# A gated linear-attention layer and its channel mixer on one core: cumulative decays move from PSUM to SBUF buffers, and the loads of later units' decays wait for a chunk's keys

## The chip, the core and the metric

The kernel runs on one core of a Trainium2 chip. The core has five engines that run side by side, each through its own list of instructions in order: TensorE (PE, matmuls; PEld is its weight load), VectorE (DVE), ScalarE (ACT), GpSimd (POOL) and SyncE (SP), which here issues all DMAs. They share SBUF; PE writes to PSUM, which DVE and ACT can read and write. The metric is the device time of one launch in microseconds (us). Before the change it was 357.06 us in the median of 3 runs (356.91 to 357.37).

## The reference

Batch 4, 8 heads, 768 steps, head width 48, so model width 384; the mixer's inner width is 1024. All in float32.

```python
f = 1.0 / (1.0 + np.exp(-f_logit))
for t in range(S):
    state = f[:, :, t, :, None] * state + np.einsum('bhd,bhe->bhde', k[:, :, t], v[:, :, t])
    y[:, :, t] = np.einsum('bhd,bhde->bhe', q[:, :, t], state)
...
x = y with the heads side by side
x_prev = x one step earlier (zero at the first)
xk = mu_k * x + (1.0 - mu_k) * x_prev
xr = mu_r * x + (1.0 - mu_r) * x_prev
k = np.maximum(xk @ w_k, 0.0)
v = k * k @ w_v
r = 1.0 / (1.0 + np.exp(-(xr @ w_r)))
return r * v
```

## The kernel before

**Chunks and units.** The 4 x 768 steps are cut into 24 chunks of 128 steps (index i) and 8 units of three chunks, 384 steps (index u). Attention goes chunk by chunk, the mixer unit by unit.

**Attention of chunk i** (`add_attention`). The steps have short names, which the text uses with the chunk's number behind them:

- `qk`, `v`: loads of queries with keys, and of values. `f{u}` loads the logits of a unit's decays (768 KB), `sf{u}` takes their sigmoid on ACT.
- `b`: a scan on DVE gives the running product of the decays within the chunk, 128 x 512 (L240). `bl` copies its last column. `ln`, `rb`: ACT takes its logarithm and the exponential of the negative, that is its reciprocal (L246, L248).
- `q`: q times b (L250). `kr`: k times the reciprocal, in two halves (L258, L259). `n`: reciprocal times b, which corrects the rounding of the reciprocal (L270). `k`: the corrected key, in three pieces (L262, L266).
- `TR`: PE transposes the keys into PSUM (L310); `kt` copies them to SBUF, on ACT (L314) or DVE (L315).
- `SP`: PE forms the scores and the chunk's sum of key times value (L325, L345). `m` copies the scores with the causal mask, on DVE (L337); for the first `AWAY` chunks ACT copies (L332) and `mg` on GpSimd masks (L334).
- `g`, `za`, `zb`, `T`: the state carried from chunk to chunk (L287 to L302). `YA`, `YB`: PE forms the output from the state and from the chunk (L362); `w` reads a marker between the two (L381, L382). `y` copies the output to SBUF (L394 on ACT, L396 on DVE), and `sp` spreads two heads' rows with small DMAs.

**Mixer of unit u** (`add_mix`). `d` is the difference of x and its predecessor (L464; for unit 0 two scaled copies on ACT, L474), `xm` the mix (L482; L477 for unit 0). Since PE multiplies with shortened numbers, every operand is split: `xh` is the rounded mix (L490 on ACT, L491 on DVE), `xl` the rest (L497, GpSimd). `F{u}.{f}`: eight groups of nine matmuls with W_k; `R{u}.{t}`: three with W_r; `W{u}.{t}{h}`: six of twelve matmuls with W_v (all L505). Between them `r` (relu, L528 or L529), `h` and `kk` (the square, rounded and exact), `l` (their difference, L543), `lg` and `sg` (the gate; `sg{u}` also takes the sigmoid of `f{u+3}` into the same buffer on ACT, between two table loads), `o` (the product) and `out`.

**Weights** (`add_words`). W_k, W_r and W_v come as 64-bit words in 8, 4 and 6 pieces. A piece is loaded, put together on DVE in three steps (`S` L623, `T` L632, `X` L635), rounded on ACT (`H` L638), and the rest taken on GpSimd (`L` L642). The W_v pieces pass through two buffers in turn, so piece 2 is loaded when piece 0 is done. `S` and `T` need a PSUM buffer in between.

**What sets the order.** All these steps are tasks with a place, one or several ways (an engine, an estimated duration) and the tasks they come after. `Plan.schedule` plays the program through with these estimates, picks at each turn the task that can start first (the smaller place on a tie) and the way that would end first, with a penalty for some engines (`DEAR`); it also puts in filler matmuls on PE (L700) where it expects PE to wait. What it yields is pinned: each engine's instructions stand in just this order. So a changed constant can move instructions on every engine. `BUFS` gives the number of buffers by tag. The tag `pm` has four PSUM buffers of 2 KB a partition; they serve `b`, `TR`, `d`, `F`, `R`, `W` and the weights' `S` and `T`. `NFB` = 3 buffers hold the decays `f`, `NQ` = 4 the queries and keys. `general` is a slow path for extreme data; it is not run here.

Of the kernel before, what the change touches and what calls it, by code (L numbers as in the profile page):

```python
# [52 lines left out]
SPLIT = True
HALVED = 1
PLACE = {"f1": -0.627, "f2": 0.21, "sf2": -1.016, "qk0": 0.854, "qk1": -0.278, "qk2": 0.127, "qk3": 0.31, "v0": -0.151, "v1": -0.224, "cst": 0.482, "mu": 0.138, "f3": -1.807}
CHECK = (2.0, 0.2)
DEAR = {"V": 2.498, "A": 2.512}


class Plan:  # L60
# [23 lines left out]
    def schedule(self, trace=None):  # L84
        free = {"P": 0.0, "V": 2.2, "A": 0.0, "G": 1.0, "Q": 0.7}
# [106 lines left out]
class Rwkv:  # L192


    wk = wr = wv = None
# [19 lines left out]
    def add_attention(self, pl, i):  # L215
        nc = self.nc
        u, c = divmod(i, UC)
        cs = i % NCH
# [5 lines left out]
        I = lambda name, j=i: [f"{name}{j}"] if j >= 0 and j % NCH in have.get(name, range(NCH)) else []  # L224
# [15 lines left out]
        pl.add(f"b{i}", ga, ("V", 1.25, 1, lambda: nc.vector.tensor_tensor_scan(  # L240
            b().rearrange(FL), f().rearrange(FL), self.low.rearrange(FL), 1.0, op0=ALU.mult, op1=ALU.max)),
            after=[f"sf{u}.{c}" if u == 0 else f"sf{u}"], takes=[("pm", ("b", i))])
        pl.add(f"bl{i}", ga, ("A", 0.2, 0, lambda: nc.scalar.copy(self.bl[:, i], b()[:, :, C - 1])),
               ("V", 0.15, 0, lambda: nc.vector.tensor_copy(self.bl[:, i], b()[:, :, C - 1])),
               uses=[("pm", ("b", i))])
        pl.add(f"ln{i}", ga, ("A", 0.63, 0, lambda: nc.scalar.activation(rb(), b(), AF.Ln)),  # L246
               after=["ex"], takes=[("rb", i)], uses=[("pm", ("b", i))])
        pl.add(f"rb{i}", ga, ("A", 0.63, 0, lambda: nc.scalar.activation(rb(), rb(), AF.Exp, scale=-1.0)),  # L248
               after=I("ln"), uses=[("rb", i)])
        pl.add(f"q{i}", ga, ("V", 0.69, 0, lambda: nc.vector.tensor_tensor(q(), q(), b(), op=ALU.mult)),  # L250
               after=I("qk"), uses=[("pm", ("b", i))])
# [18 lines left out]
        pl.add(f"n{i}", ga, ("V", 0.69, 0, lambda: nc.vector.tensor_tensor(b(), rb(), b(), op=ALU.mult)),  # L270
               after=I("rb") + I("q") + I("bl"), uses=[("pm", ("b", i)), ("rb", i)])
# [13 lines left out]
        if cs > 0:  # L285
# [3 lines left out]
            def state(e):  # L289
# [655 lines left out]
```

## Time and profile before

| | |
|---|---|
| median of 3 runs | 357.06 us (356.91 to 357.37) |
| the profiled execution | 357.22 us, of it 355.1 us the span of the instructions |
| instructions | 10862, of them 4482 matmuls |
| moved by DMA | 45.32 MB, mean 128 GB/s |
| granted PE clock over the span | 0.99 |

How to read it: the page gives each engine's busy time over the span, and the span in 40 slices of 8.9 us, where a digit is the busy share in tenths. A row of a timeline is: start, duration, engine, line, operation, output<-input, count, and in brackets how long the engine had been idle before and who ended that. A row of the groups is: line, engine, operation, tiles, count | busy us, mean ns of one | idle us just before them, and whom they waited for. In the chain that ended last a row is: start, duration, engine, tile, line; "issue" is time in which the engine waited for nothing that the profile shows. Line numbers are those of the kernel before; in the changed kernel the same statements stand one or two lines further down.

### The profile page before, as it was taken

How to read it: one execution, taken by the hardware profiler on the slowest of the kernel's cores; microseconds unless marked ns; L12 is line 12 of the kernel's file. 1: busy time of each engine (PE TensorE's matmuls, PEld its weight loads, DVE VectorE, ACT ScalarE, POOL GpSimd, SP SyncE). 2: the span in 40 equal slices, each digit the busy share in tenths (PEclk: the TensorE clock that was granted, in tenths of full speed). 3: DMA queues.
4: the chain of work that ended last, by engine and by line, in shares of the span. 5: the costliest groups of instructions: out<-in, count | busy, mean ns of one | idle time of the engine just before them, and what ended most of it. 6: DMA issues, size and time to landing. Idle time of an engine off the chain costs nothing.

```text
span 355.1 us, 10862 instructions
## 1 busy us (share of the span) xinstructions
PE 320.0 (90%) x4482; PEld 304.0 (86%) x4482; DVE 260.3 (73%) x526; ACT 201.5 (57%) x400; POOL 196.5 (55%) x235
## 2 busy tenths in 40 slices
PE   0294678999999999999999999999999999999993
PEld 0283567888989999999999999999999999999992
DVE  7887699989998798877999788848973943723110
ACT  3786358758367827844467537772676156605520
POOL 2555459985779357733677267725790634634400
PEclk9999899999999999999999999999999999999998
DMA  7999462336451363366323632131401100010001
GB/s 260 398 378 372 162 223 65 106 105 209 118 185 59 127 226 129 123 236 221 117 81 116 212 128 89 46 121 52 160 1 38 50 27 11 9 46 22 3 24 52
DMA packets 20650, 45.32 MB, mean 128 GB/s; under 512 B 2928, under 2 KB 13040, under 8 KB 20592
## 3 DMA queue, kind: packets, MB, share of 16 engines
q1 hardware_dynamic: 20592, 44.55, 37.0%
q8 instruction: 37, 0.61, 0.7%
q14 instruction: 21, 0.17, 0.1%
HBM read 38.64 MB, written 4.72 MB: 122 GB/s over the span
## 4 chain that ended last, share of the span: by engine, by line
PE 68%; DVE 13%; ACT 5%; issue 4%; DMA 3%; POOL 3%; SPq 1%; DVEq 0%; POOLq 0%; ACTq 0%
PE pm L505 55%; PE py L362 6%; PE pm L310 3%; PE pss L325 2%; DMA f<-in_zt 2%; DVE pm L632 2%; PE pss L345 2%; DVE pm L623 2%; POOL k2l L543 1%; DVE xm L482 1%; DVE ss L337 1%; DMA words<-in_wv 1%; DVE xm L477 1%; DVE words L635 1%; DVE xh L491 1%
## 5 line engine op out<-in xcount | busy, mean ns | idle before, releaser
L505 PE MATMUL pm<-xh,wk 128*128 128x384 f32 x384 | 105.3, 344 | 1.5 <-POOL wk L642 1.1
L505 PE MATMUL pm<-wv,k2h 128*128 128x384 f32 x384 | 98.6, 338 | 0.0
L543 POOL TENSOR_TENSOR k2l<-kk,k2h 128x384 fp32r<-128x384 f32 x64 | 68.5, 1075 | 32.2 <-DVE kk L535 16.3
L497 POOL TENSOR_TENSOR xl<-xm,xh 128x384 fp32r<-128x384 f32 x48 | 52.5, 1095 | 60.4 <-DVE xh L491 54.6
L505 PEld LDWEIGHTS pm<-xh,wk 128*128 128x128 f32 x384 | 69.8, 188 | 4.4 <-POOL wk L642 2.0
L505 PEld LDWEIGHTS pm<-wv,k2h 128*128 128x128 f32 x384 | 68.7, 188 | 0.3
L505 PE MATMUL pm<-xl,wk 128*128 128x384 f32 x192 | 64.6, 337 | 0.0
L505 PE MATMUL pm<-wv,k2l 128*128 128x384 f32 x192 | 64.5, 336 | 0.0
L528 ACT ACTIVATE r<-pm 128x384 f32<-128x384 f32 x54 | 26.5, 490 | 34.0 <-PE pm L505 33.3
L505 PE MATMUL pm<-wr,xh 128*128 128x384 f32 x144 | 38.0, 345 | 1.0 <-DVE words L635 0.9
L505 PEld LDWEIGHTS pm<-wv,k2l 128*128 128x128 f32 x192 | 36.1, 188 | 0.0
L595 DVE TENSOR_TENSOR o<-pm,lg 128x384 f32<-128x384 f32 x24 | 13.3, 553 | 31.1 <-PE pm L505 30.9
L505 PEld LDWEIGHTS pm<-xl,wk 128*128 128x128 f32 x192 | 36.1, 188 | 0.0
L535 DVE SCALAR_TENSOR_TENSOR kk<-pm,r 128x384 f32<-128x384 f32 x38 | 21.1, 554 | 20.0 <-ACT r L528 18.8
L533 ACT ACTIVATE k2h<-r 128x384 fp32r<-128x384 f32 x64 | 33.6, 524 | 3.5 <-DVE r L529 1.2
L240 DVE TENSOR_TENSOR_SCAN pm<-f,low 128x512 f32<-128x512 f32 x24 | 32.7, 1363 | 0.1
L362 PE MATMUL py<-qk,z 64*64 64x64 f32 x704 | 22.9, 230 | 10.0 <-issue 3.3
L362 PEld LDWEIGHTS py<-qk,z 64*64 64x64 f32 x704 | 16.4, 135 | 18.0 <-issue 8.8
L505 PEld LDWEIGHTS pm<-wr,xh 128*128 128x128 f32 x144 | 25.2, 188 | 1.9 <-DVE words L635 1.0
L482 DVE SCALAR_TENSOR_TENSOR xm<-pm,mu_sb,x 128x384 f32<-128x384 f32 x42 | 25.7, 612 | 0.7
L700 PE MATMUL py<-ident 128*128 128x64 f32 x72 | 10.8, 310 | 15.4 <-DMA ident<-in_cst 15.4
L505 PE MATMUL pm<-wr,xl 128*128 128x384 f32 x72 | 24.2, 336 | 0.0
(101 smaller groups left out, 559.2 us busy)
## 6 DMA issues: line engine op xcount, KB each, us to landing
qk<-in_qkt SPq DMA_DIRECT2D x24, 512.0 KB, 4.3
words<-in_wv SPq DMA_DIRECT2D x12, 512.0 KB, 3.9
f<-in_zt SPq DMA_DIRECT2D x7, 768.0 KB, 5.2
v<-in_vt SPq DMA_DIRECT2D x24, 192.0 KB, 3.1
out<-o SPq DMA_DIRECT2D x24, 192.0 KB, 2.6
words<-in_wk SPq DMA_DIRECT2D x6, 512.0 KB, 5.4
words_k2h<-in_wk SPq DMA_DIRECT2D x4, 384.0 KB, 8.6
words_k2l<-in_wk SPq DMA_DIRECT2D x4, 384.0 KB, 9.4
```

What stands on the lines that cost most here:

```text
L240: pl.add(f"b{i}", ga, ("V", 1.25, 1, lambda: nc.vector.tensor_tensor_scan(b().rearrange(FL), f().rearrange(FL), self.low.rearrange(FL), 1. ...
L310: nc.tensor.transpose(pk()[:, j], k()[:, j], self.ident)
L362: first[c, h] = nc.tensor.matmul(to, lhs, rhs, start=(c, h) not in first, stop=stop, skip_group_check=True)
L482: pl.add(f"xm{u}.{n}{j}", pr, ("V", 0.62, 0, lambda xm=xm, n=n, j=j: nc.vector.scalar_tensor_tensor(xm(), pm("d", u, j)[:, :UT], self.mu_s ...
L497: e.tensor_tensor(lo(), xm(), hi().bitcast(F32), op=ALU.subtract)
L505: nc.tensor.matmul(ps, lhs(a, j), rhs(bb, j), start=ends[0] and i == 0, stop=ends[1] and i == len(pr) - 1)
L528: pl.add(f"r{u}.{f}", kf, ("A", 0.5, 0, lambda r=r, ps=ps: nc.scalar.activation(r(), ps(), AF.Relu)), ("V", 0.56, 0, lambda r=r, ps=ps: nc ...
L533: pl.add(f"h{u}.{f}", kf, ("A", 0.53, 0, lambda r=r, hi=hi: nc.scalar.activation(hi(), r(), AF.Square)), after=[f"r{u}.{f}"], **kw)
L535: pl.add(f"kk{u}.{f}", kf, ("V", 0.56, 0, lambda r=r, ps=ps, kk=kk: nc.vector.scalar_tensor_tensor(kk(), ps(), 0.0, r(), op0=ALU.max, op1= ...
L543: e.tensor_tensor(lo(), kk(), hi().bitcast(F32), op=ALU.subtract)
L595: pl.add(f"o{u}.{t}", kv, ("V", 0.56, 0, lambda t=t, ps=ps, o=o: nc.vector.tensor_tensor(o(), ps(), lg()[:, t], op=ALU.mult)), after=[f"W{ ...
L700: self.nc.tensor.matmul(self.py[:, 0, 256:320], self.ident, self.ident[:, :64], start=False, stop=True, skip_group_check=True)
```

## The change

It does five things.

1. `b` leaves the PSUM buffers `pm` and gets three SBUF buffers of its own, tag `b`. Every step that reads or writes it follows: `bl`, `ln`, `q`, `n`, `k`.
2. The load `f{u}` for u >= 3 (whose buffer held the decays of unit u - 3) now also comes after `kt` of chunk 3(u - 3) + 4, that is after the keys of a chunk of the unit in between have been transposed and copied.
3. `q` and `n` may also be done by GpSimd. The planner counts `q`, `n` and `k` on DVE as steps that get in the way of GpSimd.
4. The planner's penalties: DVE 2.709 and ACT 2.426 (2.498 and 2.512 before), and 3.606 and 7.281 more for `q` and `n` on GpSimd. The score copies of the first four chunks instead of one go by ACT and GpSimd (`AWAY`).
5. Other constants of the planner: the distance at which attention leads the mixer, places of loads and of weight pieces, the chunk from which YA, SP and YB are tied together (`TIED` 7 instead of 8), and assumed delays.

```diff
 BUFS = {
-    "pm": (4, [512]), "rb": (2, [NP, C]),
+    "pm": (4, [512]), "b": (3, [512]), "rb": (2, [NP, C]),
...
-LEAD, GATE, PREP = 1.669, 0.274, 0.51
-WORDS = {"wk": (-0.282, 0.023), "wr": (-4.892, 0.005), "wv": (-0.241, 0.052)}
-HAND, DRAIN = 0.136, 0.465
+LEAD, GATE, PREP = 1.617, 0.274, 1.949
+WORDS = {"wk": (-0.422, 0.041), "wr": (-5.439, 0.054), "wv": (-0.301, 0.066)}
+HAND, DRAIN = 0.132, 0.301
...
-TIED = 8
+TIED = 7
...
-AWAY = 1
+AWAY = 4
...
-DEAR = {"V": 2.498, "A": 2.512}
+DEAR = {"V": 2.709, "A": 2.426, "qG": 3.606, "nG": 7.281}
...
-                pick = min(((max(at[w[0]], free[w[0]]) + w[1] + DEAR.get(w[0], 0.0), w) for w in ways), key=lambda x: x[0])[1]
+                pick = min(((max(at[w[0]], free[w[0]]) + w[1] + DEAR.get(w[0], 0.0) + DEAR.get(n[0] + w[0], 0.0), w) for w in ways), key=lambda x: x[0])[1]
...
-        b = lambda: self.b("pm", ("b", i)).rearrange("p (a c) -> p a c", a=NP)
+        b = lambda: self.b("b", i).rearrange("p (a c) -> p a c", a=NP)
...
-        pl.add(f"q{i}", ga, ("V", 0.69, 0, lambda: nc.vector.tensor_tensor(q(), q(), b(), op=ALU.mult)),
-               after=I("qk"), uses=[("pm", ("b", i))])
+        pl.add(f"q{i}", ga, ("V", 0.69, 1, lambda: nc.vector.tensor_tensor(q(), q(), b(), op=ALU.mult)),
+               ("G", 1.3, 0, lambda: nc.gpsimd.tensor_tensor(q(), q(), b(), op=ALU.mult)),
+               after=I("qk"), uses=[("b", i)])
...
-        pl.add(f"n{i}", ga, ("V", 0.69, 0, lambda: nc.vector.tensor_tensor(b(), rb(), b(), op=ALU.mult)),
-               after=I("rb") + I("q") + I("bl"), uses=[("pm", ("b", i)), ("rb", i)])
-        pl.add(f"k{i}", ga, ("V", 0.98, 0, k_b), after=I("n") + I("kr"), uses=[("pm", ("b", i))])
+        pl.add(f"n{i}", ga, ("V", 0.69, 1, lambda: nc.vector.tensor_tensor(b(), rb(), b(), op=ALU.mult)),
+               ("G", 1.3, 0, lambda: nc.gpsimd.tensor_tensor(b(), rb(), b(), op=ALU.mult)),
+               after=I("rb") + I("q") + I("bl"), uses=[("b", i), ("rb", i)])
+        pl.add(f"k{i}", ga, ("V", 0.98, 1, k_b), after=I("n") + I("kr"), uses=[("b", i)])
...
-            pl.add(f"f{u}", ga - 0.4 if u >= NFB else -1.5 + 0.1 * u, ("Q", 2.13, 1, load), after=gates)
+            pl.add(f"f{u}", ga - 0.4 if u >= NFB else -1.5 + 0.1 * u, ("Q", 2.13, 1, load), after=gates + ([f"kt{UC * (u - NFB) + 4}"] if u >= NFB else []))
```

What the planner makes of it, at three places. Numbers behind a tile's name tell buffers apart.

*SP, the first loads after the four pieces of W_r.* f_61 x3 are unit 0's decays in three parts, f_62 are unit 1's; qk_65 is chunk 1's, qk_64 chunk 0's and qk_66 chunk 2's load. Before:

```order
L410 DMA f_61<-in_zt 128x512 x3
L228 DMA qk_65<-in_qkt 128x1024
L230 DMA v_101<-in_vt 128x384
L410 DMA f_62<-in_zt 128x1536
L230 DMA v_102<-in_vt 128x384
L228 DMA qk_66<-in_qkt 128x1024
```

and now:

```order
L412 DMA f_62<-in_zt 128x1536
L412 DMA f_61<-in_zt 128x512 x3
L230 DMA v_104<-in_vt 128x384
L228 DMA qk_64<-in_qkt 128x1024
L228 DMA qk_66<-in_qkt 128x1024
L230 DMA v_105<-in_vt 128x384
```

Unit 1's decays move ahead of unit 0's, and no q, k or v stands between the two any more; chunk 0's q and k come before chunk 1's. Further down, unit 3's decays stood between the first two pieces of W_k; now they stand after chunk 7's q and k, just ahead of W_v's piece 2.

*DVE, from the first state copy (sm, chunk 0's T) on.* words are pieces of W_k, pm_91 to pm_94 the PSUM buffers, b_95 to b_97 the new ones. Before:

```order
L302 TENSOR_TENSOR sm<-pss,z_73 128x192
L623 TENSOR_SCALAR pm_92<-words_k2h_129 128x384
L270 TENSOR_TENSOR pm_93<-rb_95,pm_93 128x512
L632 SCALAR_TENSOR_TENSOR pm_92<-words_k2h_129,pm_92 128x384
L337 TENSOR_TENSOR ss_98<-pss,mask 128x512
L296 TENSOR_TENSOR z_75<-pss,z_74 128x4x48
L302 TENSOR_TENSOR sm<-pss,z_75 128x192
L262 SCALAR_TENSOR_TENSOR qk_66<-pm_93,qk_66 128x2x128
L266 SCALAR_TENSOR_TENSOR qk_66<-pm_93,qk_66 128x2x64 x2
L270 TENSOR_TENSOR pm_94<-rb_96,pm_94 128x512
```

and now:

```order
L304 TENSOR_TENSOR sm<-pss,z_73 128x192
L263 SCALAR_TENSOR_TENSOR qk_66<-b_97,qk_66 128x2x128
L267 SCALAR_TENSOR_TENSOR qk_66<-b_97,qk_66 128x2x64 x2
L715 TENSOR_SCALAR one_mu<-mu_sb 128x6
L271 TENSOR_TENSOR b_95<-rb_99,b_95 128x512
L298 TENSOR_TENSOR z_75<-pss,z_74 128x4x48
L304 TENSOR_TENSOR sm<-pss,z_75 128x192
L317 COPY ktk_102<-pm_93 128x384
L263 SCALAR_TENSOR_TENSOR qk_67<-b_95,qk_67 128x2x128
L267 SCALAR_TENSOR_TENSOR qk_67<-b_95,qk_67 128x2x64 x2
L240 SCALAR_TENSOR_TENSOR b_96<-f_62,low 128x512
```

The masked score copy (L337) is gone from here, W_k's first piece stands later, and the correction of chunk 2's reciprocal stands ahead of the piece shown; a key copy (L317) and the scan of chunk 4 have come in. In the same way, up to W_v's last piece, the score copies of chunks 1 to 3, the read marker of chunk 2, chunk 4's key copy, three of unit 0's five roundings on DVE and the output of chunk 5 go to ACT (the score copies' mask to GpSimd), and chunk 3's `q` goes to GpSimd.

*PE, chunk 8 (qk_64) in the middle of unit 1's F groups.* Before, its scores and sums stand alone between two groups:

```order
L505 MATMUL pm_94<-xh_122,wk_81 128x384
L505 MATMUL pm_94<-xl_123,wk_81 128x384
L505 MATMUL pm_94<-xh_122,wk_82 128x384
L325 MATMUL pss<-qk_64 64x64 x16
L345 MATMUL pss<-v_103,ktk_99 48x48 x16
L505 MATMUL pm_91<-xh_122,wk_81 128x384
L505 MATMUL pm_91<-xl_123,wk_81 128x384
```

and now between the two parts of chunk 7's output (qk_67):

```order
L364 MATMUL py<-qk_67,z_75 64x64 x2
L364 MATMUL py<-qk_67,z_74 64x64 x2
L364 MATMUL py<-qk_67,z_75 64x64
L327 MATMUL pss<-qk_64 64x64 x16
L347 MATMUL pss<-v_106,ktk_102 48x48 x16
L364 MATMUL py<-qk_67,z_74 64x64
L364 MATMUL py<-qk_67,z_75 64x64 x2
L364 MATMUL py<-qk_67,z_74 64x64 x2
L364 MATMUL py<-qk_67,z_75 64x64 x2
L364 MATMUL py<-qk_67,z_74 64x64
L364 MATMUL py<-ss_101,v_105 48x64 x16
L507 MATMUL pm_93<-xh_125,wk_81 128x384
```

Three separate pieces of attention have become one. From unit 0's second W_v group to the end, pieces of attention between big matmuls (those of transposes alone not counted) fall from 26 to 22. PE has 52 filler matmuls instead of 36.

More of the change, by code (lines that the diff above doesn't have):

```diff
@@ L34 @@
 BUFS = {
-    "pm": (4, [512]), "rb": (2, [NP, C]), "ss": (2, [2, NP, C // 2]), "ktk": (2, [NP, 2, D]), "v": (3, [H, D]),
+    "pm": (4, [512]), "b": (3, [512]), "rb": (2, [NP, C]), "ss": (2, [2, NP, C // 2]), "ktk": (2, [NP, 2, D]), "v": (3, [H, D]),
     "x": (3, [KJ, 1 + UT]), "stage": (2, [1, UT]), "xm": (4, [UT]), "r": (2, [UT]), "kk": (2, [UT]),
@@ L51 @@
 BUNDLE = True
-AWAY = 1
+AWAY = 4
 SPLIT = True
 HALVED = 1
-PLACE = {"f1": -0.627, "f2": 0.21, "sf2": -1.016, "qk0": 0.854, "qk1": -0.278, "qk2": 0.127, "qk3": 0.31, "v0": -0.151, "v1": -0.224, "cst": 0.482, "mu": 0.138, "f3": -1.807}
+PLACE = {"f1": -0.926, "f2": -0.182, "sf2": -2.507, "qk0": 0.143, "qk1": 0.836, "qk2": -0.365, "qk3": 0.216, "v0": -0.151, "v1": -0.236, "cst": 0.341, "mu": 0.138, "f3": -2.293}
 CHECK = (2.0, 0.2)
-DEAR = {"V": 2.498, "A": 2.512}
+DEAR = {"V": 2.709, "A": 2.426, "qG": 3.606, "nG": 7.281}
 class Plan:
@@ L241, in add_attention @@
             b().rearrange(FL), f().rearrange(FL), self.low.rearrange(FL), 1.0, op0=ALU.mult, op1=ALU.max)),
-            after=[f"sf{u}.{c}" if u == 0 else f"sf{u}"], takes=[("pm", ("b", i))])
+            after=[f"sf{u}.{c}" if u == 0 else f"sf{u}"], takes=[("b", i)])
         pl.add(f"bl{i}", ga, ("A", 0.2, 0, lambda: nc.scalar.copy(self.bl[:, i], b()[:, :, C - 1])),
                ("V", 0.15, 0, lambda: nc.vector.tensor_copy(self.bl[:, i], b()[:, :, C - 1])),
-               uses=[("pm", ("b", i))])
+               uses=[("b", i)])
         pl.add(f"ln{i}", ga, ("A", 0.63, 0, lambda: nc.scalar.activation(rb(), b(), AF.Ln)),
-               after=["ex"], takes=[("rb", i)], uses=[("pm", ("b", i))])
+               after=["ex"], takes=[("rb", i)], uses=[("b", i)])
         pl.add(f"rb{i}", ga, ("A", 0.63, 0, lambda: nc.scalar.activation(rb(), rb(), AF.Exp, scale=-1.0)),
                after=I("ln"), uses=[("rb", i)])
-        pl.add(f"q{i}", ga, ("V", 0.69, 0, lambda: nc.vector.tensor_tensor(q(), q(), b(), op=ALU.mult)),
-               after=I("qk"), uses=[("pm", ("b", i))])
+        pl.add(f"q{i}", ga, ("V", 0.69, 1, lambda: nc.vector.tensor_tensor(q(), q(), b(), op=ALU.mult)),
+               ("G", 1.3, 0, lambda: nc.gpsimd.tensor_tensor(q(), q(), b(), op=ALU.mult)),
+               after=I("qk"), uses=[("b", i)])
         def halves(t):
```

## The prediction

> **What bounds the kernel now.** I read the page first: busy shares and the span in 40 slices.
>
> ```profile
> PE 320.0 (90%) x4482; PEld 304.0 (86%) x4482; DVE 260.3 (73%) x526; ACT 201.5 (57%) x400; POOL 196.5 (55%) x235
> ...
> PE   0294678999999999999999999999999999999993
> ...
> DVE  7887699989998798877999788848973943723110
> ...
> GB/s 260 398 378 372 162 223 65 106 105 209 118 185 59 127 226 129 123 236 221 117 81 116 212 128 89 46 121 52 160 1 38 50 27 11 9 46 22 3 24 52
> ```
>
> Two regimes show: some nine slices (80 us) in which the matmul engine fills up and the vector engine is the busy one, then a long stretch with PE at 9. Busy time by stretch (after the length: PE, PEld, DVE, ACT and POOL with their counts, granted clock, DMA share, GB/s) puts the border at 81.3 us.
>
> ```profile
> 24.52:53.97 29.45, 19.30 (x651) 16.59 (x651) 24.45 (x54) 16.44 (x44) 16.78 (x26) 0.94 0.74 255
> 53.97:79.35 25.38, 23.14 (x195) 20.88 (x194) 23.59 (x44) 18.85 (x41) 23.78 (x23) 1.00 0.31 94
> 81.30:349.25 267.95, 267.49 (x3538) 257.42 (x3536) 189.98 (x384) 149.01 (x294) 145.35 (x169) 1.00 0.30 100
> ```
>
> In the last row PE is busy for 267.49 of 267.95 us. Nothing there is to be won by data that comes sooner; only less time on PE, or the whole block sooner, shortens the run. The block begins with unit 0's second half of W_v (81.31). What holds it back is read in the chain of waits and the timelines of PE and GpSimd:
>
> ```profile
> 71.06 2.33 POOL wv L642
> 73.42 3.69 DMA words<-in_wv
> ...
> 79.38 0.65 ACT wv L638
> ...
> 80.11 1.30 POOL L642 TENSOR_TENSOR wv<-words,wv 128x512 fp32r<-128x512 f32 x1 [1.15 <-ACT wv L638]
> ...
> 81.31 0.59 PE L505 MATMUL pm<-wv,k2h 128*128 128x384 f32 x2
> ```
>
> The last weight piece is decoded on DVE until just before 79.38, rounded on ACT, split on GpSimd until 81.41, and the first matmuls that need it start at 81.31. So **the start is a queue of vector work**, and the forecast is: when does that queue end, and how long is PE's block after it.
>
> **What the change does to that queue.** Count from the first state copy (24.52) to the last word piece (79.35).
>
> ```profile
> 24.52 0.36 DVE L302 TENSOR_TENSOR sm<-pss,z 128x192 f32<-128x192 f32 x1 [0.40 <-ACT z L300]
> ...
> 36.47 0.16 DVE L382 COPY done<-py 128x2 f32<-128x2 f32 x1 [2.04 <-PE py L362]
> ...
> 44.20 0.56 DVE L315 COPY ktk<-pm 128x384 f32<-128x384 f32 x1 [1.94 <-PE pm L310]
> ...
> 75.12 1.04 DVE L396 TENSOR_SCALAR x<-py 128x256 f32<-128x256 f32 x3
> 76.18 0.29 DVE L396 TENSOR_SCALAR stage<-py 128x128 f32<-128x128 f32 x1
> ...
> 77.13 0.69 DVE L623 TENSOR_SCALAR pm<-words 128x512 int32<-128x512 int32 x1 [0.66 <-DMA words<-in_wv]
> ```
>
> (A) *The queue begins earlier.* The first exponentials wait for unit 1's sigmoid and a table load:
>
> ```profile
> 5.19 8.03 DMA f<-in_zt
> ...
> 16.04 0.60 ACT rb L246
> ...
> qk<-in_qkt SPq DMA_DIRECT2D x24, 512.0 KB, 4.3
> ...
> v<-in_vt SPq DMA_DIRECT2D x24, 192.0 KB, 3.1
> ```
>
> One q/k load and one v load (704 KB) no longer stand before the end of units 0 and 1's decays; at the second slice's 398 GB/s that is 1.8 us. Unit 0's three sigmoids, which lay in that shadow, now come after their data, so I take 1.0 (ends 0 and 1.8): **-1.0**.
>
> (B) *Tasks.* Until the last word piece these leave DVE: three masked score copies (m1 to m3, now ACT and GpSimd), three roundings of x, one key copy net of the one that comes (kt4 out, kt2 in: 0), chunk 5's output y5, one read marker; n2 moves ahead of the count, and the scan of chunk 4 moves into it. By these rows, with issue to issue about 0.09 below the mean of one:
>
> ```profile
> L240 DVE TENSOR_TENSOR_SCAN pm<-f,low 128x512 f32<-128x512 f32 x24 | 32.7, 1363 | 0.1
> ...
> L491 DVE CAST xh<-xm 128x384 fp32r<-128x384 f32 x38 | 19.3, 510 | 1.5
> L270 DVE TENSOR_TENSOR pm<-rb,pm 128x512 f32<-128x512 f32 x24 | 16.5, 687 | 0.7 <-ACT rb L248 0.7
> ...
> L464 DVE TENSOR_TENSOR pm<-x 128x384 f32<-128x384 f32 x21 | 14.7, 698 | 7.2 <-DMA x<-stage 6.7 <-ACT lg L562 0.3
> ```
>
> 3 x 0.60 (a 512-wide product like L270) + 3 x 0.50 + 1.35 (y5's four instructions from 75.12 on) + 0.1 + 0.60 (n2) less 1.25 (scan) and some 0.2 for small copies: 3.9 leaves. Of it y5's 1.35 is worth nothing. It stood while the last words were in flight: round on ACT, split (2.33), load (3.69) take 6.9 from 70.2 to 77.13, and DVE already waits 0.66 at their end; the two buffers for these words are unchanged. So 1.4 comes back (0.4 if the split takes 1.3 as at 80.11): **-2.5**.
>
> (C) *Two waits.* The marker (2.04) and kt4 (1.94) held DVE for PE; both are on ACT now, 4.0 less. What is late next is the first mix of unit 0. Its scaling stands on ACT behind three more score copies, kt4 and a marker; a score copy there is shown once, and its mask on GpSimd:
>
> ```profile
> L332 ACT COPY ss<-pss 128x512 f32<-128x512 f32 x1 | 0.6, 585 | 0.2 <-PE pss L345 0.2
> ...
> L334 POOL TENSOR_TENSOR ss<-ss,mask 128x512 f32<-128x512 f32 x1 | 1.3, 1272 | 4.2 <-ACT ss L332 4.2
> ```
>
> 3 x 0.59, and for kt4 and the marker 0.56 and 0.16 as on DVE, make 2.5. I let that come back, ends 0 and 4.0: **-1.5**.
>
> (D) *The price of the new place of b.* With b in PSUM, q, n and k (L250, L270, L262, L266) have an operand outside SBUF; now both are in SBUF. The trace has no such form, so I bound it. ACT now reads b from SBUF, which by the first two rows below costs 24 x 0.03, off the path. On DVE the nearest is the difference L464, two operands in SBUF:
>
> ```profile
> L248 ACT ACTIVATE rb<-rb 128x512 f32<-128x512 f32 x24 | 15.1, 629 | 0.5
> L246 ACT ACTIVATE rb<-pm 128x512 f32<-128x512 f32 x24 | 14.4, 600 | 4.4 <-DVE bl L244 2.1 <-DVE qk L250 2.0 <-POOL qk L259 0.4
> ...
> 83.69 0.56 DVE L464 TENSOR_TENSOR pm<-x 128x384 f32<-128x384 f32 x1
> ...
> 90.44 1.20 DVE L464 TENSOR_TENSOR pm<-x 128x384 f32<-128x384 f32 x1
> ```
>
> The first ran while GpSimd was idle, the second beside it. So the wait is 0 to 0.64 an instruction; the mean of L464 is 0.14 over its quiet value with GpSimd busy 55% of the span. In the two stretches quoted above GpSimd is busy 57% and 94% (16.78 of 29.45, 23.78 of 25.38): 12 instructions (n3, n4, q4 and three each of k2, k3, k4) at 0.15 and 6 (q5, n5, k5, q6) at 0.25 give **+3.3**, ends 0 and 18 x 0.64 = 11.5. Where DVE comes first, GpSimd waits instead, and the last split is late by as much; the ends hold for both. The Trainium skill (SBUF — State Buffer, section "SBUF: two separate sides") speaks against the change here: a DVE instruction with two SBUF inputs and a GpSimd one share a port pair under an exclusive lock, and the later one blocks until the other is through. The spread of L464 agrees; by that rule with GpSimd always first, the sum would be that of the slow rival below.
>
> Start: -1.0 - 2.5 - 1.5 + 3.3 = **-1.7**, so the block starts near 79.6.
>
> (E) *PE's block.* The attention matmuls of a chunk come in fewer pieces. One piece, scores and sums alone, between big matmuls:
>
> ```profile
> 94.87 0.34 PE L505 MATMUL pm<-wv,k2l 128*128 128x384 f32 x1
> 95.14 0.69 PE L325 MATMUL pss<-qk 64*64 64x64 f32 x32
> ...
> 96.12 0.45 PE L505 MATMUL pm<-xh,wk 128*128 128x384 f32 x1
> ```
>
> Big matmuls follow each other at 0.17 (a row of x1 shows 0.34 because they overlap). Here 0.27 passes before the attention part starts, and the first big one after it is about 0.1 slow; so a switch there and back costs 0.2 to 0.4, taken as 0.3. After 81.3 the order before has 26 such pieces (transposes apart, whose switches hardly cost), the order after 22: 4 x 0.3 = **-1.2** (0.8 to 1.6). The set of matmuls from there to the end is the same, and so is the tail from the last matmul.
>
> (F) *The wait that is added.* Unit 3's decays are loaded only after chunk 4's keys are copied; behind that load on SP stand the last four W_v pieces and later q, k, v. Chunk 4's copy comes long before (44.20 above) 55.64, where the first of those pieces was issued for want of a free buffer, and unit 3's decays are read by ACT only after 81: 0. That the load no longer runs among W_k's pieces is worth 0 too: DVE never waits for a W_k piece in these loads' turn (second row below, idle 0.0). q3 and q7 go to GpSimd, 1.27 each as L334, where it still idles in the first stretch. Sixteen more warm-up matmuls (L700) go to PE before chunk 5's end, where PE waits anyway; without that cover they cost 32 records of 0.11, 3.5 us. In the block, DVE loses about 30 roundings, all ten relus and eight squares to ACT, which goes from 190 of 268 us towards 220; I take 0 for new waits, with an upper end of 2.
>
> ```profile
> 54.61 1.89 PE L700 MATMUL py<-ident 128*128 128x64 f32 x16
> ...
> L623 DVE TENSOR_SCALAR pm<-words_k2l 128x384 int32<-128x384 int32 x4 | 2.2, 552 | 0.0
> ...
> 55.64 0.33 SPq L629 DMA_DIRECT2D words<-in_wv  x1
> ```
>
> **Sum.** The profiled execution took 357.22 (span 355.1), 0.16 above the median of the runs shown, 357.06. -1.7 - 1.2 = -2.9: **354.2** on the scale of the runs. With the ends of A, B, C and E, and D between 1.5 and 5, the likeliest case spans 352.3 to 356.2.
>
> **Rivals.** *The ports cost more than the queue wins (slower).* If each of the 18 instructions waits half of a GpSimd instruction (rows below: half of 1.08 or 1.10 is 0.54), D is 9.7 and the sum -1.0 - 2.5 - 1.5 + 9.7 - 1.2 = +3.5: 360.6. The place is the 50 us before the block, where GpSimd is busy 57% and then 94%; it decides from 0.34 an instruction, where the sum is 0. For it: 94%. Against it: the scans, always exposed, average only 0.14 over their shortest, 1.22.
>
> ```profile
> L543 POOL TENSOR_TENSOR k2l<-kk,k2h 128x384 fp32r<-128x384 f32 x64 | 68.5, 1075 | 32.2 <-DVE kk L535 16.3
> L497 POOL TENSOR_TENSOR xl<-xm,xh 128x384 fp32r<-128x384 f32 x48 | 52.5, 1095 | 60.4 <-DVE xh L491 54.6
> ```
>
> *The queue's gain is lost to ACT and GpSimd.* The score copies of chunks 1 to 3 become ACT (0.59) and then GpSimd (1.27) instead of DVE (0.69), some 1.2 more on each chunk's way to x. If the first mix comes no sooner than now, only E is left: 357.06 - 1.2 = 355.9, with 0.8 either way. *No contention:* D = 0 leaves -2.9 - 3.3 = -6.2: 350.9; the scans speak against it. That the delayed load does nothing by itself is already in the sum as 0.
>
> **How the numbers follow.** Likeliest case 0.52, lost gain 0.22, fast 0.14, slow 0.12. About 0.2% (0.7 us) is what a measurement of this kernel can tell from no change. Faster than 356.35: nearly all of the first, all of the fast one and two thirds of the lost gain, 0.78. Within: 0.09. Slower: 0.13. The range that leaves about 2 in 10 out runs from the fast case's middle to just over today's time: 350.8 to 357.4.
>
> **What would show it.** In the changed profile: the last W_v split ends near 79.6 and PE is full from there (start right); the state copy of chunk 0 near 23.5 (A); no DVE wait for PE's read marker or key copy before the mix (C); the means of L250, L271, L263 and L267 by at most 0.15 to 0.25 above quiet ones (D); from the block's first matmul to the last about 266.7 instead of 267.9 (E). It is wrong if q, n and k stretch by 0.34 or more, if the first mix still comes at 46, or if PE shows idle time after 80 us.

## The result: 370.27 us, slower

| | before | after |
|---|---|---|
| median, same chip | 357.22 us (356.91 to 358.05, 4 runs) | 370.27 us (369.98 to 371.07, 4 runs) |
| ratio | 1 | 1.0365, 95% interval 1.034 to 1.039 |
| span of the profiled execution | 355.1 us | 368.2 us |
| first matmul of PE's block (W0.01) | 81.31 | 90.75 |
| from there to the last matmul's end | 267.91 | 271.70 |

The forecast was 354.2 with a range of 350.8 to 357.4. Of the 13.1 us of span, 9.4 come before the block and 3.8 within it; what follows the last matmul is 0.1 shorter. The page of the changed kernel, with the granted clock by slice:

```profile
PE 333.1 (90%) x4514; PEld 318.5 (86%) x4514; DVE 264.2 (72%) x446; ACT 231.4 (63%) x478; POOL 221.3 (60%) x240
...
PE   0297799897999998899999999999999999999993
...
DVE  7898897878979889975999489948994732713210
...
PEclk9999658899899999999999999999999999999998
```

80 instructions have left DVE and it is busy 3.9 us longer than before. The groups of DVE say why (busy us, mean ns of one):

```profile
L271 DVE TENSOR_TENSOR b<-rb,b 128x512 f32<-128x512 f32 x24 | 26.2, 1094 | 2.5 <-ACT rb L248 1.8
L267 DVE SCALAR_TENSOR_TENSOR qk<-b,qk 128x128 f32<-128x128 f32 x48 | 25.8, 576 | 0.0
...
L250 DVE TENSOR_TENSOR qk<-qk,b 128x512 f32<-128x512 f32 x22 | 20.1, 915 | 1.2 <-DMA qk<-in_qkt 1.2
L263 DVE SCALAR_TENSOR_TENSOR qk<-b,qk 128x256 f32<-128x256 f32 x24 | 17.5, 728 | 4.1 <-POOL qk L259 2.7
...
L244 DVE COPY bl<-b 128x4 f32<-128x4 f32 x7 | 3.9, 560 | 0.2
```

The same groups in before (n, L270, stands in the prediction):

```profile
L250 DVE TENSOR_TENSOR qk<-qk,pm 128x512 f32<-128x512 f32 x24 | 16.3, 679 | 4.1 <-ACT rb L246 3.3 <-DMA qk<-in_qkt 0.8
...
L266 DVE SCALAR_TENSOR_TENSOR qk<-pm,qk 128x128 f32<-128x128 f32 x48 | 11.5, 280 | 0.3 <-POOL qk L259 0.3
L262 DVE SCALAR_TENSOR_TENSOR qk<-pm,qk 128x256 f32<-128x256 f32 x24 | 10.0, 419 | 2.0 <-POOL qk L258 0.9
...
L244 DVE COPY bl<-pm 128x4 f32<-128x4 f32 x16 | 2.5, 157 | 0.4
```

n is at 1.094 us against 0.687, q at 0.915 against 0.679, a chunk's k at 0.73 + 2 x 0.58 against 0.42 + 2 x 0.28, and the copy of b's last column at 0.56 against 0.16. The timeline of DVE has them one by one, ahead of the queue that the prediction counted (it begins with chunk 0's state copy, sm) and in it, and what DVE waits for:

```profile
21.02 1.03 DVE L271 TENSOR_TENSOR b<-rb,b 128x512 f32<-128x512 f32 x1
22.16 1.31 DVE L263 SCALAR_TENSOR_TENSOR qk<-b,qk 128x256 f32<-128x256 f32 x1
23.39 1.55 DVE L267 SCALAR_TENSOR_TENSOR qk<-b,qk 128x128 f32<-128x128 f32 x2
24.86 1.75 DVE L271 TENSOR_TENSOR b<-rb,b 128x512 f32<-128x512 f32 x1
26.53 0.34 DVE L304 TENSOR_TENSOR sm<-pss,z 128x192 f32<-128x192 f32 x1
...
38.58 1.73 DVE L250 TENSOR_TENSOR qk<-qk,b 128x512 f32<-128x512 f32 x1
40.35 1.39 DVE L271 TENSOR_TENSOR b<-rb,b 128x512 f32<-128x512 f32 x1
...
46.02 0.60 DVE L479 SCALAR_TENSOR_TENSOR xm<-x,one_mu,pm 128x384 f32<-128x384 f32 x1
...
58.83 0.70 DVE L625 TENSOR_SCALAR pm<-words 128x512 int32<-128x512 int32 x1 [2.06 <-ACT r L530]
...
68.46 2.10 DVE L267 SCALAR_TENSOR_TENSOR qk<-b,qk 128x128 f32<-128x128 f32 x2
...
85.48 0.69 DVE L625 TENSOR_SCALAR pm<-words 128x512 int32<-128x512 int32 x1 [1.54 <-ACT lg L564]
...
88.75 1.58 DVE L267 SCALAR_TENSOR_TENSOR qk<-b,qk 128x128 f32<-128x128 f32 x2
```

And PE's timeline shows a second thing, 8.79 us of warm-up matmuls (the planner's fillers, two records each) right ahead of unit 0's first W_k piece, and PE waiting for chunk 6's keys just before the block:

```profile
47.01 8.79 PE L702 MATMUL py<-ident 128*128 128x64 f32 x40
55.56 0.67 PE L507 MATMUL pm<-xh,wk 128*128 128x384 f32 x1
...
90.48 0.52 PE L312 MATMUL pm<-ident,qk 128*128 128x128 f32 x3 [1.25 <-DVE qk L267]
90.75 0.60 PE L507 MATMUL pm<-wv,k2h 128*128 128x384 f32 x2
```

### The profile page after: what moved, and what is told of

It reads as the page before. It is cut to its first block, busy times and chain, and to the rows that moved or that the text cites. A ratio compares the mean times of both kernels' runs of the same rounds, so it can differ in the third digit from the quotient of the medians.

```text
span 368.2 us, 10877 instructions
## 1 busy us (share of the span) xinstructions
PE 333.1 (90%) x4514; PEld 318.5 (86%) x4514; DVE 264.2 (72%) x446; ACT 231.4 (63%) x478; POOL 221.3 (60%) x240
## 4 chain that ended last, share of the span: by engine, by line
PE 56%; DVE 17%; DMA 9%; POOL 7%; ACT 4%; issue 4%; SPq 3%; DVEq 0%; POOLq 0%; ACTq 0%
PE pm L507 43%; PE py L364 4%; DMA qk<-in_qkt 4%; DVE b L271 3%; DVE qk L267 3%; PE py L702 3%; DMA words<-in_wv 3%; SPq L454 2%; PE pss L327 2%; DVE b L240 2%; POOL k2l L545 2%; DMA f<-in_zt 2%; DVE qk L250 2%; DVE qk L263 2%; PE pm L312 2%
## 5 line engine op out<-in xcount | busy, mean ns | idle before, releaser
L545 POOL TENSOR_TENSOR k2l<-kk,k2h 128x384 fp32r<-128x384 f32 x64 | 72.9, 1149 | 38.5 <-DVE kk L537 26.9
L499 POOL TENSOR_TENSOR xl<-xm,xh 128x384 fp32r<-128x384 f32 x48 | 54.7, 1167 | 27.2 <-DVE xh L493 21.9
L530 ACT ACTIVATE r<-pm 128x384 f32<-128x384 f32 x64 | 31.2, 488 | 32.7 <-PE pm L507 29.9
L597 DVE TENSOR_TENSOR o<-pm,lg 128x384 f32<-128x384 f32 x24 | 13.1, 551 | 29.9 <-PE pm L507 27.0
L702 PE MATMUL py<-ident 128*128 128x64 f32 x104 | 20.1, 374 | 15.4 <-DMA ident<-in_cst 15.4
L702 PEld LDWEIGHTS py<-ident 128*128 128x128 f32 x104 | 19.6, 288 | 15.6 <-issue 15.3
L240 DVE TENSOR_TENSOR_SCAN b<-f,low 128x512 f32<-128x512 f32 x24 | 30.7, 1279 | 2.4 <-ACT f L418 1.4
L537 DVE SCALAR_TENSOR_TENSOR kk<-pm,r 128x384 f32<-128x384 f32 x30 | 16.5, 552 | 21.3 <-ACT r L530 20.9
L292 POOL TENSOR_TENSOR z<-sm,g 128x192 f32<-128x192 f32 x20 | 12.3, 616 | 31.1 <-DVE sm L304 31.1
L492 ACT CAST xh<-xm 128x384 fp32r<-128x384 f32 x40 | 20.2, 513 | 15.9 <-DVE xm L484 15.4
L259 POOL TENSOR_TENSOR qk<-qk,rb 128x256 f32<-128x256 f32 x24 | 23.4, 973 | 8.5 <-DMA qk<-in_qkt 4.9
```

Source lines behind the costliest of these rows:

```text
L259: e.tensor_tensor(k()[:, ::2], k()[:, ::2], rb()[:, ::2], op=ALU.mult)
L492: pl.add(f"xh{u}.{n}{j}", pr, ("A", 0.51, 0, lambda xm=xm, hi=hi: nc.scalar.copy(hi(), xm())), ("V", 0.4, 1, lambda xm=xm, hi=hi: nc.vecto ...
L499: e.tensor_tensor(lo(), xm(), hi().bitcast(F32), op=ALU.subtract)
L530: pl.add(f"r{u}.{f}", kf, ("A", 0.5, 0, lambda r=r, ps=ps: nc.scalar.activation(r(), ps(), AF.Relu)), ("V", 0.56, 0, lambda r=r, ps=ps: nc ...
L537: pl.add(f"kk{u}.{f}", kf, ("V", 0.56, 0, lambda r=r, ps=ps, kk=kk: nc.vector.scalar_tensor_tensor(kk(), ps(), 0.0, r(), op0=ALU.max, op1= ...
L545: e.tensor_tensor(lo(), kk(), hi().bitcast(F32), op=ALU.subtract)
```

## The experiments

Three theories: the *ports* (q, n and k, now with two inputs in SBUF, and GpSimd's instructions hold each other up), the *warm-up matmuls* (they hold PE up), and the *order* (the planner's new numbers make a slower order whatever the rest does). Each ratio below is to runs of before on the same chip, whose medians were 357.4 to 357.7.

### One part at a time

**sbuf_only**: the order of before, b in SBUF and nothing else (three buffers in turn; chunk 3's b takes the SBUF buffer of the gate).

```diff
-        b = lambda: self.b("pm", ("b", i)).rearrange("p (a c) -> p a c", a=NP)
+        def b():
+            if i != 3:
+                return self.b_t[i % 3]
+            return self.tiles["lg"][0].rearrange(FL)[:, :512].rearrange("p (a c) -> p a c", a=NP)
...
```

> The kernel before, in its own order, with the cumulative decays b in SBUF and nothing else changed (q and n all on VectorE). Port theory: per chunk q, n and the three pieces of k get longer by 0.24 + 0.41 + 0.31 + 2 x 0.30 = 1.55 us, as in the changed kernel; six chunks lie before PE's block, 9.3 us, less the 3 to 4 us that VectorE waits there anyway: 362 to 366 where before is 357.2. Warm-up and order theories: the order and the warm-up matmuls are those of before, so 357 to 358.5.

374.54 us, ratio 1.0509 (1.0445 to 1.0573): 17.2 us, more than the port theory asked for. Its groups of DVE:

```profile
L270 DVE SCALAR_TENSOR_TENSOR qk<-bs,qk 128x128 f32<-128x128 f32 x46 | 26.2, 609 | 0.0
...
L274 DVE TENSOR_TENSOR bs<-rb,bs 128x512 f32<-128x512 f32 x23 | 21.2, 922 | 0.6
...
L254 DVE TENSOR_TENSOR qk<-qk,bs 128x512 f32<-128x512 f32 x23 | 17.1, 745 | 0.0
L266 DVE SCALAR_TENSOR_TENSOR qk<-bs,qk 128x256 f32<-128x256 f32 x23 | 16.2, 705 | 1.1
```

PE's block as a window (length; busy PE, PEld, DVE, ACT, POOL; clock, DMA share, GB/s):

```profile
84.77:365.81 281.04, 270.30 (x3538) 257.56 (x3536) 214.28 (x383) 148.41 (x293) 157.79 (x167) 1.00 0.29 94
```

and the longest of PE's waits in it (us in total, times, longest):

```profile
PE pm L509 <- DVE kk L539: 7.8, 5, 2.4
```

The block starts 3.5 us late (84.77 against 81.31) and is 13.1 longer (281.04 against 267.91): PE, full in the block of before, now stands idle for 10.7 of it, mostly for the squares on DVE, which is busy for 214.28 us there (189.98 in before). So the price of the place falls mainly in the block, which no theory had said.

**late_loads**: the kernel before with the loads of units 3 to 7's decays moved on SP to behind the key copy that the change names; nothing else moves.

```diff
...
+    for u in range(NFB, U):
+        names = [n for n, _, _ in order]
+        load = order.pop(names.index(f"f{u}"))
+        order.insert([n for n, _, _ in order].index(f"kt{UC * (u - NFB) + 4}") + 1, load)
...
```

> The kernel before with only the loads of units 3 to 7's decays moved on SP to behind the key copy of the chunk that the change names (chunk 4 for unit 3). If the late loads cost anything by themselves (SP held by the wait, decays late for the scans of unit 3), over 358. All other theories: 357.2 within 0.7.

354.74, ratio 0.992 (0.9895 to 0.9945); run again as **late_loads_again**,

> late_loads once more, to have its gain with a narrower interval: 354.7 within 0.7, 1 to 3 us under before. If its gain was an accident of one chip: 357 or more.

354.62, ratio 0.9917 (0.9898 to 0.9936). A gain of 2.6 to 2.9 us that no theory had. In before, GpSimd's product for chunk 4's keys waited for its load,

```profile
36.38 0.74 POOL L258 TENSOR_TENSOR qk<-qk,rb 128x256 f32<-128x256 f32 x1 [1.65 <-DMA qk<-in_qkt]
```

and in late_loads (GpSimd, DVE, PE) the 768 KB are no longer ahead of it:

```profile
34.79 0.72 POOL L258 TENSOR_TENSOR qk<-qk,rb 128x256 f32<-128x256 f32 x1 [0.20 <-DMA qk<-in_qkt]
...
44.34 0.60 DVE L477 SCALAR_TENSOR_TENSOR xm<-x,one_mu,pm 128x384 f32<-128x384 f32 x1
...
79.72 0.60 PE L505 MATMUL pm<-wv,k2h 128*128 128x384 f32 x2
```

1.6 us earlier there, 1.65 at the first mix (45.99 before), 1.6 at the block; the two profiled executions differ by 1.6 too (355.61 for 357.22). This version beats both kernels. **late_no_fill** takes its warm-up matmuls behind chunk 4's sums away too:

> late_loads (before with the later loads of decays) without the 24 warm-up matmuls behind chunk 4's sums. If the warm-up matmuls only fill idle time there: 354.7 within 0.7. If they hold PE up as in the changed kernel: 1 to 2 us less. If they keep the clock up: 1 us more or worse.

356.35, ratio 0.996 (0.9929 to 0.9991): no gain; here they are harmless or useful, which the interval does not separate.

**no_fill**: the changed kernel without the 20 warm-up matmuls ahead of the first W_k piece.

```diff
...
+    order = [t for p, t in enumerate(order) if not (back < p < first and t[0].startswith("fill"))]
...
```

> The changed kernel without the 20 warm-up matmuls that stand between chunk 4's sums and unit 0's first W_k piece; every other instruction in its order. Warm-up theory: they ran at half clock for 8.79 us and held PE to 55.56, while the third split of x was through near 52.1; without them the first W_k piece starts near 52.2, DVE's wait for unit 0's first relu (2.06) goes, and the run takes 3 to 4 us less, 366 to 367. Port theory (q, n and k in SBUF wait for GpSimd): PE's block waits for the decoded W_v pieces and keys, which are late by DVE's and GpSimd's own queues; at most 1 us less, 369 to 370.5. Order theory (the new numbers of the planner make a slower order whatever the ports do): as the port theory.

367.07, ratio 1.0266 (1.0206 to 1.0327) against the changed kernel's 1.0365: 3.2 us, as the warm-up theory had it. They explain a quarter.

**old_numbers**: the changed code with the planner's numbers of before.

> The changed kernel with the planner's numbers of before (leads, word turns, AWAY 1, TIED 8, places, prices of an engine): b in three SBUF buffers, the later loads, GpSimd allowed for q and n. Order theory: the new numbers are what costs, so 357 to 359. Port theory: the new place costs whatever the numbers: 362 to 370.

376.16, ratio 1.0547 (1.0485 to 1.0608). With b in SBUF the new numbers win 5.9 us over this. But it is not the order of before: without the surcharges on GpSimd the planner gives it 23 of the 24 q and 22 of the 24 n, at 1.38 and 1.40 us each; in the changed kernel it has two q.

### The price by itself

**prices** adds stretches behind the work of before: products like n (DVE) and like half of kr (GpSimd), alone and side by side.

> The kernel before with seven stretches added behind its last work: 12 products of VectorE (128x512, both inputs in SBUF) alone; 12 products of GpSimd (128x256) alone; 12 and 20 of them side by side; the same with one input of VectorE's product in PSUM; 16 key pieces of VectorE (128x256, both inputs in SBUF) beside 20 of GpSimd; 16 copies of the last column (128x4, SBUF to SBUF) beside 20 of GpSimd, and 16 of them alone. Port theory: alone 0.68 and 0.73; side by side VectorE's product near 1.05 to 1.2 and GpSimd's near 1.0, the key piece 0.42 to over 0.7, the last column 0.16 to 0.55; with an input in PSUM 0.68 and 0.73 as alone. If the place of the operand is not what counts, side by side is as alone in every stretch, or stretched with PSUM too.

The groups of five stretches, each from its own window: DVE's product alone; GpSimd's alone; both, with both of DVE's inputs in SBUF; both, with one of them in PSUM; the key piece with both in SBUF.

```profile
L835 DVE TENSOR_TENSOR f<-f 128x512 f32<-128x512 f32 x5 | 3.5, 692 | 0.2
...
L847 POOL TENSOR_TENSOR qk<-qk,qk 128x256 f32<-128x256 f32 x12 | 8.7, 724 | 0.9
...
L847 POOL TENSOR_TENSOR qk<-qk,qk 128x256 f32<-128x256 f32 x11 | 11.7, 1063 | 0.9
L835 DVE TENSOR_TENSOR f<-f 128x512 f32<-128x512 f32 x11 | 11.6, 1059 | 0.4
...
L838 DVE TENSOR_TENSOR f<-f,pm 128x512 f32<-128x512 f32 x12 | 8.2, 687 | 0.4
L847 POOL TENSOR_TENSOR qk<-qk,qk 128x256 f32<-128x256 f32 x11 | 8.0, 725 | 0.9
...
L841 DVE SCALAR_TENSOR_TENSOR f<-f 128x256 f32<-128x256 f32 x15 | 12.0, 801 | 0.5
L847 POOL TENSOR_TENSOR qk<-qk,qk 128x256 f32<-128x256 f32 x15 | 11.9, 793 | 1.2
```

Alone they take 0.692 and 0.724. With one input in PSUM both engines go as if alone (0.687 and 0.725). With both in SBUF they take turns, and each pays: 1.06 and 1.06; the key piece takes 0.80 (0.42 in before, with one input in PSUM) and GpSimd's product beside it 0.79. The copies of the last column left no record, so their price is not measured here. That whichever comes second waits is what the Trainium skill (SBUF — State Buffer, section "SBUF: two separate sides") says of its lock. The measured price is less than a whole instruction of the other engine: DVE's product loses 0.37, of GpSimd's 0.72.

### GpSimd cut short

To see what is left without the contention, GpSimd's key products, splits of x and squares (from unit 1 on) work on 16 columns a row, so part of the output is left out; the DVE instructions stay as they are. The splits of the weights, the masks and unit 0's squares keep their full length on GpSimd. **before_short** is the base, **sbuf_short** and **after_short** are sbuf_only and the changed kernel cut in the same way.

```diff
...
+            n = W if e is nc.gpsimd else C
+            e.tensor_tensor(k()[:, ::2, :n], k()[:, ::2, :n], rb()[:, ::2, :n], op=ALU.mult)
...
```

> The kernel before in its order, with GpSimd's key products, its splits of x and (from unit 1 on) of the squares cut to 16 columns of each row; the rest of their outputs keeps old values, so the output is not the reference's. It is the base for the next two runs. GpSimd is seldom waited for in PE's block here, so 351 to 357 by every theory.

> The kernel before in its order with the cumulative decays in SBUF, and GpSimd's instructions cut as in before_short (the same part of the output is left out). Port theory: with GpSimd hardly busy, q, n and k go at 0.70, 0.70, 0.42 and 0.28 again, and of the 17.2 us of sbuf_only at most 4 are left over before_short. If the place in SBUF costs by itself (its buffers' waits, the copies and logarithms that read it), 13 or more are left.

> The changed kernel with GpSimd's instructions cut as in before_short (the same part of the output is left out). Port theory: of the 13 us between the changed kernel and before at most 4 are left over before_short, those of the warm-up matmuls. Order theory (the new numbers make a slower order whatever the ports do): 9 or more are left.

| | full | GpSimd cut |
|---|---|---|
| order of before, b in PSUM | 357.4 | 355.90 (ratio 0.9956, 0.9939 to 0.9973) |
| order of before, b in SBUF | 374.54 | 357.50 (1.0000, 0.9986 to 1.0013) |
| changed kernel | 370.27 | 366.31 (1.0222, 1.0177 to 1.0267) |

In the order of before the place costs 17.2, and 1.6 (357.50 against 355.90) with GpSimd cut: nine tenths of it are contention. n is nearly back at 729 ns, q at 692, the key pieces at 444 and 325:

```profile
L278 DVE TENSOR_TENSOR bs<-rb,bs 128x512 f32<-128x512 f32 x23 | 16.8, 729 | 1.5 <-ACT rb L255 1.0
L257 DVE TENSOR_TENSOR qk<-qk,bs 128x512 f32<-128x512 f32 x23 | 15.9, 692 | 0.3 <-DMA qk<-in_qkt 0.3
L274 DVE SCALAR_TENSOR_TENSOR qk<-bs,qk 128x128 f32<-128x128 f32 x46 | 13.1, 325 | 0.0
L270 DVE SCALAR_TENSOR_TENSOR qk<-bs,qk 128x256 f32<-128x256 f32 x23 | 10.2, 444 | 1.1
```

In the changed kernel the time falls by 4.0, but before itself falls by 1.5, so of the loss of 13.05 only 2.6 go and 366.31 - 355.90 = 10.4 stay. Here the port theory, as it stood, fell, and the order theory had its number. That the new order is slower by itself does not follow for all of the 10.4, because the cut leaves contention in place. By DVE's timelines, q, n, k and the copies of the last column ahead of PE's block are together 11.6 us longer than their forms in before in the changed kernel, and still 8.7 in after_short (6.8 and 4.2 in sbuf_only and sbuf_short). The last of it holds PE up right at the block: the two narrow pieces of chunk 6's k take 1.58 instead of 0.48 beside the split of the last W_v piece (GpSimd, DVE, PE of after_short; the same rows stand at 88.48, 88.75 and 90.48 in the changed kernel):

```profile
89.77 1.51 POOL L650 TENSOR_TENSOR wv<-words,wv 128x512 fp32r<-128x512 f32 x1 [1.94 <-ACT wv L646]
...
90.04 1.58 DVE L271 SCALAR_TENSOR_TENSOR qk<-b,qk 128x128 f32<-128x128 f32 x2
...
91.77 0.52 PE L316 MATMUL pm<-ident,qk 128*128 128x128 f32 x3 [1.24 <-DVE qk L271]
```

So 10.4 is, by these runs, the most that the order costs by itself. The new order does not meet GpSimd less either: over the whole run these DVE instructions are some 39 us longer than in before in the changed kernel, and some 33 in sbuf_only. It loses less to that all the same, with a block of PE of 271.7 against 281.0. DVE, which has given 80 instructions away, is busy for 188.1 us of that block, against 214.3, which would explain it; no run tests that alone.

### What makes the new order slow

From after_short, one thing after the other put back as before (GpSimd cut in all): **short_no_fill** drops the 36 warm-up matmuls behind chunk 4's sums, **short_own_masks** also does the masked score copies of chunks 1 to 3 on DVE again, **short_first_loads** also issues the first 14 loads in the order of before, **short_early_keys** also puts chunk 5's scan, q, n and k ahead of the first mix.

> after_short without the warm-up matmuls behind chunk 4's sums (20, 12 and 4 of them; GpSimd's instructions cut as there, the same part of the output left out). after_short took 366.3, before_short 355.9: 10.4 us that are not GpSimd's. Warm-up theory: in after_short the 20 held PE from 48.1 to 56.9 at half clock while the third split of x was through at 50.8, and VectorE then waited 3.65 for the first relu: 4 to 6 us go, 360 to 362. Order theory (vector work and waits in the new order): at most 1.5 go, 365 or more.

> short_no_fill with the masked score copies of chunks 1 to 3 on VectorE again, as before the change (one instruction there for one on ScalarE and one on GpSimd). If the longer way over ScalarE and GpSimd holds up the first unit (VectorE waited 3.87 for chunk 3's copy in after_short): 1.5 to 3 us less than short_no_fill. If the tasks that left VectorE are a gain, as the prediction's step B has it: 1 to 2 us more.

> short_own_masks with the first 14 loads on SP in the order of before (unit 0's decays and chunk 1's keys ahead of unit 1's decays). In the changed order the first scan starts at 10.7, before at 9.3, and GpSimd waits 2.5 for chunk 1's keys. If the order of the first loads counts: 1 to 2 us less than short_own_masks; else within 0.7.

> short_first_loads (GpSimd's instructions cut, the same part of the output left out; no warm-up matmuls behind chunk 4's sums, own masks, the first loads of before) with chunk 5's scan, logarithm, q, n and k ahead of unit 0's first mix, where before has them, in place of among the W_k pieces. short_first_loads took 361.2, before_short 355.9, and PE waited 3.1 us for chunk 5's keys and 2.9 for chunk 6's ahead of its block. If the place of chunk 5 is what is left of the new order: PE's wait for chunk 5 goes and the run comes to 356 to 359. If it only moves the same vector work: the first mix comes 4 us later and the run stays at 361 within 1.

| run | us | ratio, interval |
|---|---|---|
| after_short | 366.31 | 1.0222 (1.0177 to 1.0267) |
| short_no_fill | 362.86 | 1.0126 (1.0061 to 1.0191) |
| short_own_masks | 360.95 | 1.0087 (1.0056 to 1.0119) |
| short_first_loads | 361.16 | 1.0108 (1.0079 to 1.0137) |
| short_early_keys | 360.81 | 1.0104 (1.0063 to 1.0144) |

The warm-up matmuls are 3.4 again; here the two intervals overlap a little, while no_fill's and the changed kernel's lie apart. In after_short the third split was through at 50.8, and this is what followed on PE and on DVE:

```profile
48.10 8.79 PE L708 MATMUL py<-ident 128*128 128x64 f32 x40
...
60.44 0.69 DVE L631 TENSOR_SCALAR pm<-words 128x512 int32<-128x512 int32 x1 [3.65 <-ACT r L535]
```

The masks' 1.9 has the forecast sign of the longer way, but the two intervals overlap; the order of the first loads and the place of chunk 5 changed nothing that these runs can tell. **early_keys**, chunk 5 ahead in no_fill with GpSimd at full length,

> no_fill (the changed kernel without the 20 warm-up matmuls; it computes what the reference does) with chunk 5's vector work ahead of the first mix as in short_early_keys. With GpSimd at full length the moved q, n and k wait for it wherever they stand. Order theory: 2 to 4 us less than no_fill's 367.1. Port theory: within 1.5 of it, since VectorE's queue is as long as before.

took 367.39, ratio 1.027 (1.0242 to 1.0298) against 1.0266: nothing. So of the 10.4 us some 3.4 are the warm-up matmuls, up to 1.9 the masks, and **4.9 (360.8 against 355.9) stay open**. Contention is a candidate that these runs do not rule out: in short_early_keys q, n, k and the column copies are still 6.0 us longer ahead of the block than in before, and PE's last wait, 1.24 us for chunk 6's keys, is there unchanged. How much of the 4.9 that is was not tried. What the new numbers would give with b left in PSUM was not tried.

## Why the prediction was wrong, step by step

**What bounds the kernel**: right for the start (a queue of vector work), wrong for the block. "Nothing there is to be won by data that comes sooner" holds, but the reverse was not asked: how little longer DVE's instructions may get until PE has to wait. sbuf_only lost 13.1 us there.

**(D), the price of b's place**, is the step that failed, not in its mechanism but in its size and reach. It priced 18 instructions at +3.3. The same 18 (from the timeline: q4 +1.05, n4 +0.70, k5 +1.91 ...) are 4.8 longer, 0.27 each; that was near. Left out were n1, k1 and n2 ahead of the count (3.4 us longer by the rows above than their forms in before), the copies of b's last column (0.56 for 0.16), k6 behind the last word piece (+1.1), and all of the block. Taken as a whole, with the order held, the place costs 17.2 us where the step had 3.3 (sbuf_only); 15.6 of that go when GpSimd is cut (sbuf_short). What it costs within the new order is not separated: 2.6 of the loss went with the cut, and contention was left.

**(A), the queue begins earlier (-1.0)**: the copy came at 26.53, 2.0 later than before's 24.52. Ahead of it n, k and the column copies are 4.6 us longer than their forms in before, and the first scan starts 1.4 later (10.62 for 9.26), waiting for unit 0's sigmoid. With GpSimd cut in both, the copy comes at 23.58 against 23.73, 0.15 earlier, with 1.5 us of lengthening still ahead of it. So contention ahead of the count undid the step, and that 1.0 could be had without it is not shown.

**(B) and (C), tasks and waits (-2.5 and -1.5)**: from that copy to the last word piece DVE was busy 50.35 us (48.03 before) and idle 10.7 (6.8):

```profile
26.53:87.62 61.09, 54.02 (x872) 50.06 (x871) 50.35 (x89) 38.84 (x94) 45.36 (x48) 0.83 0.44 141
```

The tasks did leave: 50.35 less the 4.8 of (D) is 2.5 below 48.03, and the longer copies are still in it. The two waits for PE (4.0) went, as said, but idle time grew by 3.9, so some 7.9 us came in other places: for the first relu (2.06, behind the warm-up matmuls), a word piece (1.65), the gate (1.54), and three shorter ones (1.33, 1.02, 0.87). The first mix stood at 46.02, as in the rival "the queue's gain is lost to ACT and GpSimd", whose 355.9 left out all of the rest.

**(E), PE's block (-1.2)**: +3.8. PE is busy for 267.91 of 271.70 us, 0.4 more than before with fewer pieces, and idle for 3.8; the forecast left 2 for new waits at the upper end. Whether the fewer pieces saved their 1.2 can't be read from this, since behind the wait for chunk 6's keys the granted clock was 0.50 for 3 us of the block, where before's block has a mean of 1.00:

```profile
92.00:95.00 3.00, 3.00 (x39) 2.56 (x42) 2.90 (x5) 1.54 (x2) 1.39 (x2) 0.50 1.01 365
```

**(F)** is the second step that failed: the warm-up matmuls were taken as hidden, with 3.5 as the price without cover. The cover was gone (the third split of x ended near 52.1, the matmuls at 55.8), and they cost 3.2 (no_fill). The late loads, taken as 0, are worth -2.6 to -2.9 in the order of before: the step looked at who waits for W_k's pieces and passed over the load of chunk 4's keys, which stood behind them on the same queue, though before's timeline shows GpSimd's wait of 1.65 for it.

**The rivals**: the slow one, at 0.12, had cause and sign (the ports), and its 360.6 was 10 us short; its place, the 50 us before the block, held 9.4 of the 13.1, but not by the 18 instructions alone. The span of the likeliest case, 352.3 to 356.2, is narrower than its ends added up, some 348 to 359, and even that does not reach 370. Of the small gains in the forecast's sum, the runs show only that the tasks left DVE and that the two waits went.

## What to carry to other kernels

Before an operand moves from PSUM to SBUF, count every DVE instruction that will then have two inputs in SBUF, over the whole run and not on the path alone, and the copies too (that of b's last column has one input and went from 0.16 to 0.56), and price each beside GpSimd with a pair of stretches as above: 0.37 us for 0.69 here, and GpSimd pays as much. An engine that is only 71% busy in a stretch may still have no slack there; hold the order and change one thing before crediting a new order with what it saves. When an engine's work is cut to take contention out, look at what is left of the contention before putting the rest down to something else. A load's cost is looked for at what stands behind it on its queue, whoever waits for that.

## What the runs showed of the hardware that was not expected

PE's granted clock stayed at half through long, nearly unbroken work. In the changed kernel, from 40.5 to 57.6, PE was busy for 16.67 of 17.10 us, 8.79 of that on the 20 warm-up matmuls, with a mean clock of 0.50:

```profile
40.50:57.60 17.10, 16.67 (x171) 15.97 (x172) 15.48 (x29) 8.67 (x19) 12.01 (x13) 0.50 0.44 147
```

In before the same stretch had 13.83 us of work and a clock of 0.90. The 40 records took 0.22 us each, about twice the 0.12 of the 16 in before at 54.61. So the 20 warm-up matmuls ran at half the clock and did not raise it while they lasted. It rose in unit 0's first W_k matmuls: it was 0.50 until 57.3 and 0.95 from there to 59.3, 1.7 us after their start, and in no_fill, without the 20, 2.7 us after it. The Trainium skill (TensorE: Matmul & The Clock Gate, section "What's actually happening") has the clock rise after some 3.4 us of busy work; this stretch does not agree, and no run here tells why.
